# Linear-attention denominators: one per chunk on the whole array, or four at once in column quarters with the reciprocals spread through DRAM

## The chip, the cores and the metric

The kernel runs on one core of a Trainium2 chip. The metric is the device time of one execution in microseconds. The kernel before took 1658.59 us (median of three runs, 1658.3 to 1659.22).

## The reference

Four layers run on x of 2048 rows by 1024: attention, gated block, attention, gated block. Each layer normalizes x without weights and adds its result to x. An attention layer computes, for 32 heads of 32 columns:

```
phi = lambda t: jnp.where(t > 0, t + 1, jnp.exp(t)) + 1e-6
pq, pk = phi(q), phi(k)
kv = jnp.einsum("bhsd,bhse->bhde", pk, v)
z = jnp.einsum("bhsd->bhd", pk)
num = jnp.einsum("bhqd,bhde->bhqe", pq, kv)
den = jnp.einsum("bhqd,bhd->bhq", pq, z)[..., None] + 1e-6
o = num / den          # then o @ wo
```

So each row and head has one denominator, the dot product of its 32 values of phi(q) with the 32 sums z of its head. A gated block computes (x @ w_gate) * (x @ w_up) @ w_down with an inner width of 3584. Weights and activations are bf16.

## The kernel before

X stays on the chip as 16 tiles of 128 rows. An attention layer has two stages. The k/v stage computes phi(k) and v for all rows and sums k-transposed times v in PSUM, with a column of ones that gives z. Behind it `finish_kv` cuts out the four 32 by 32 head blocks of each 128-column chunk with `mask`, writes z into the same block pattern as `zb` (128 x 128 per chunk), and `fold` multiplies the blocks with wo, so that the output projection and the numerator become one product with M.

The q stage is a written-out order of steps i, and it is the part that changes. A q chunk is 128 columns of q (four heads) for a group of 512 rows; there are four groups of eight chunks, 32 in all. Per step the code issues, in this order:

- `den_step` (L283) for chunk i - 4: one matmul of the chunk's `zb` with its phi(q), whose 128 output rows are each head's denominator 32 times over (`dps`); logarithm and exponential with scale -1 on ScalarE give the reciprocal `r` (L288, L289); a multiplication on VectorE gives the scaled chunk `pqs` (L292);
- `q_step` (L272) for chunk i: eight matmuls, then `phi` (L171): an exponential on ScalarE, two steps on VectorE;
- in the steps 4 to 11 one `fold` (two matmuls, one copy of M on ScalarE, one on VectorE);
- from step 12 on an `out_step` (L294): eight matmuls of the scaled chunks of a group with M, and an addition to X on VectorE.

Every engine takes its instructions in the order of the code. Products of q and output steps share four PSUM tiles (`mm`), folds and denominators three (`kv`). SyncE's queue issues the loads of the gated block's weights where `preload_B` is called (steps 0, 14, 17, 25, 33), as slots come free, and the transposes of the next layer's first rows. The gated block (L356) follows at once.

Of the kernel before, what the change touches and what calls it, by code (L numbers as in the profile page):

```python
# [9 lines left out]
ALU = mybir.AluOpType  # L10
BF16 = mybir.dt.bfloat16
F32 = mybir.dt.float32
# [3 lines left out]
def kernel(  # L16
# [11 lines left out]
    nc = tc.nc  # L28
    P = 128
# [3 lines left out]
    KD = D // P  # L33
    KF = F // P
    G = 512
    NG = S // G
    TPG = G // P
    NB = 512
    FB = F // NB
    FPB = NB // P  # L40
    DC = D // NB
    HC = 7

    ctx.enter_context(tc.manual_schedule())

# [3 lines left out]
    wp = ctx.enter_context(tc.tile_pool(name="wp", bufs=13))  # L49
    hp = ctx.enter_context(tc.tile_pool(name="hp", bufs=4))  # L50
    work = ctx.enter_context(tc.tile_pool(name="work", bufs=2))
    psum = ctx.enter_context(tc.tile_pool(name="psum", bufs=4, space=bass.MemoryType.PSUM))

    x_view = A_x[0].rearrange("(t p) d -> p t d", p=P)
# [51 lines left out]
    nc.gpsimd.memset(mask[:], 0.0)  # L106
    for b in range(4):
        nc.gpsimd.memset(mask[32 * b:32 * b + 32, 32 * b:32 * b + 32], 1.0)
    eps5 = const.tile([P, 1], F32, tag="eps5", name="eps5")
    nc.gpsimd.memset(eps5[:], 1e-5)  # L110
    eps6 = const.tile([P, 1], F32, tag="eps6", name="eps6")
# [59 lines left out]
    def phi(ps, dst):  # L171
        m = work.tile([P, NB], F32, tag="m", name="m", bufs=3)
        nc.scalar.activation(out=m[:], in_=ps[:], func=ACT.Exp)  # L173
        nc.vector.tensor_scalar(out=m[:], in0=m[:], scalar1=1.0, scalar2=1e-6, op0=ALU.min, op1=ALU.add)  # L174
        nc.vector.scalar_tensor_tensor(out=dst, in0=ps[:], scalar=0.0, in1=m[:], op0=ALU.max, op1=ALU.add)

    def layer_A(li, preload_B):
# [55 lines left out]

        kvm = work.tile([P, KD, P], BF16, tag="kvm", name="kvm", bufs=1)
        kvT = work.tile([P, KD, P], BF16, tag="kvT", name="kvT", bufs=1)
        zb = work.tile([P, KD, P], BF16, tag="zb", name="zb", bufs=1)
        z = work.tile([P, KD], F32, tag="z", name="z", bufs=1)

        def finish_kv():
            for b in range(3):  # L240
                nb = min(3, KD - 3 * b)
                src = kvp[b][:, 0:nb * VW].rearrange("p (c f) -> p c f", f=VW)
                nc.vector.tensor_copy(out=z[:, 3 * b:3 * b + nb], in_=src[:, :, P])
                for j in range(nb):
                    nc.vector.tensor_tensor(out=kvm[:, 3 * b + j, :], in0=src[:, j, 0:P], in1=mask[:], op=ALU.mult)
            for c in range(KD):
                nc.vector.tensor_scalar(out=zb[:, c, :], in0=mask[:], scalar1=z[:, c:c + 1], scalar2=None,
                                        op0=ALU.mult)

        def tr_kv():  # L250
# [15 lines left out]
                else:  # L266
                    nc.vector.tensor_copy(out=M[n][:, c, :], in_=ps[:])

        pq = {}
        pqs = {}  # L270

        def q_step(g, c):  # L272
            xnT = xnTs[(li, g)]
            w = wA["q"][c // (NB // P)]
            j = c % (NB // P)
            ps = mm_tile()
            for k in range(KD):
                nc.tensor.matmul(out=ps[:], lhsT=w[:, k, j * P:(j + 1) * P], rhs=xnT[:, k, :],  # L278
                                 start=(k == 0), stop=(k == KD - 1))
            pq[(g, c)] = work.tile([P, G], BF16, tag="pq", name="pq", bufs=6)  # L280
            phi(ps, pq[(g, c)][:])

        def den_step(g, c):  # L283
            p = pq.pop((g, c))
            dps = kv_tile("dps")
            nc.tensor.matmul(out=dps[:], lhsT=zb[:, c, :], rhs=p[:], start=True, stop=True)  # L286
            r = work.tile([P, G], F32, tag="r", name="r", bufs=2)
            nc.scalar.activation(out=r[:], in_=dps[:], func=ACT.Ln, bias=eps6[:], scale=1.0)  # L288
            nc.scalar.activation(out=r[:], in_=r[:], func=ACT.Exp, scale=-1.0)  # L289
            if c % 4 == 0:  # L290
                pqs[(g, c // 4)] = hp.tile([P, HC, G], BF16, tag="h", name="pqs")
            nc.vector.tensor_tensor(out=pqs[(g, c // 4)][:, c % 4, :], in0=p[:], in1=r[:], op=ALU.mult)  # L292

        def out_step(g, j):  # L294
            tl, n = divmod(j, DC)
            t = g * TPG + tl
            ps = mm_tile("ops")
            for c in range(KD):
                nc.tensor.matmul(out=ps[:], lhsT=pqs[(g, c // 4)][:, c % 4, tl * P:(tl + 1) * P],  # L299
                                 rhs=M[n][:, c, :], start=(c == 0), stop=(c == KD - 1))  # L300
            nc.vector.tensor_tensor(out=X[:, t, n * NB:(n + 1) * NB], in0=X[:, t, n * NB:(n + 1) * NB],
                                    in1=ps[:], op=ALU.add)

        LAG, OLAG = 4, 12
        NQ = NG * KD
        for i in range(NQ + OLAG):
            if i >= LAG and i - LAG < NQ:
                den_step(*divmod(i - LAG, KD))
            if i < NQ:
                q_step(*divmod(i, KD))  # L310
            if i == 0:
                for t in range(NT - TPG, NT):
                    kp(t)
                finish_kv()
                preload_B("p")
            if i == 3:
                tr_kv()
            if 4 <= i < 4 + KD:
                fold(i - 4)
            if i >= OLAG:  # L320
                out_step(*divmod(i - OLAG, KD))
            if i in (14, 17, 25, 33):
                preload_B({14: "pr", 17: "r", 25: "r", 33: "rrr"}[i])
            for u in range(TPG):
                if i == 20 + 2 * u:
                    ln_stats(li + 1, (u,))
                if i == 21 + 2 * u:
                    ln_norm(li + 1, u)
                if i == 22 + 2 * u:
                    tr_tile(li + 1, u)  # L330
# [25 lines left out]
    def layer_B(li, stream):  # L356
        last = li == 3
        for g in range(NG):
            xnT = xnTs[(li, g)]
            hT = []  # L360
            nl, ng = (li, g + 1) if g + 1 < NG else (li + 1, 0)
            for f in range(KF):
                fb, j = divmod(f, FPB)
                if j == 0:
                    wg, wu = stream.have.pop((g, fb))
                gp = mm_tile("gp")
                for k in range(KD):
                    nc.tensor.matmul(out=gp[:], lhsT=wg[:, k, j * P:(j + 1) * P], rhs=xnT[:, k, :],  # L368
                                     start=(k == 0), stop=(k == KD - 1))
                up = mm_tile("up")  # L370
                for k in range(KD):
                    nc.tensor.matmul(out=up[:], lhsT=wu[:, k, j * P:(j + 1) * P], rhs=xnT[:, k, :],  # L372
                                     start=(k == 0), stop=(k == KD - 1))
                gs = work.tile([P, NB], F32, tag="gs", name="gs", bufs=2)
                nc.scalar.copy(out=gs[:], in_=gp[:])  # L375
                if f % HC == 0:
                    hT.append(hp.tile([P, HC, G], BF16, tag="h", name="hT"))
                nc.vector.tensor_tensor(out=hT[f // HC][:, f % HC, :], in0=gs[:], in1=up[:], op=ALU.mult)  # L378
                if j == FPB - 1:
                    stream.pair()  # L380
                    stream.rows()
                for u in range(TPG if nl < 4 else 0):
                    t = ng * TPG + u
                    if f == 6 + 4 * u:
                        ln_stats(nl, (t,))
                    if f == 7 + 4 * u:
                        ln_norm(nl, t)
                    if f == 8 + 4 * u:
                        tr_tile(nl, t)
            xnTs.pop((li, g))  # L390
            if g == NG - 1 and not last:
                wA["k"] = load_A(1)
                wA["v"] = load_A(2)
                wA["q"] = load_A(0)
                wA["o"] = load_wo()
            for tl in range(TPG):
                t = g * TPG + tl
                for n in range(DC):
                    ps = kv_tile("dn")
                    for f in range(KF):  # L400
                        nc.tensor.matmul(out=ps[:], lhsT=hT[f // HC][:, f % HC, tl * P:(tl + 1) * P],  # L401
                                         rhs=stream.wd[f // 4][:, f % 4, n * NB:(n + 1) * NB],
                                         start=(f == 0), stop=(f == KF - 1))
                    nc.vector.tensor_tensor(out=X[:, t, n * NB:(n + 1) * NB], in0=X[:, t, n * NB:(n + 1) * NB],  # L404
                                            in1=ps[:], op=ALU.add)
                    if last:
                        nc.sync.dma_start(out=o_view[:, t, n * NB:(n + 1) * NB], in_=X[:, t, n * NB:(n + 1) * NB])
# [40 lines left out]
```

## Time and profile before

| what | value |
|---|---|
| median of three runs | 1658.59 us (1658.3 to 1659.22) |
| profiled execution, its own time | 1658.14 us |
| its span, first to last instruction | 1656.3 us |
| TensorE busy | 1644.8 us, 99% |
| VectorE busy | 558.8 us, 34% |
| ScalarE busy | 367.8 us, 22% |
| DMA packets, share of 16 engines | 35.9% |
| granted TensorE clock | 1.000 |

A group row of the profile names the line, the engine, the operation, output and inputs with their sizes, and the count; behind the first bar stand the busy time in us and the mean ns of one; behind the second the idle time of that engine just before these instructions, and what ended it. A matmul's own duration overlaps the next one's, so the pitch from start to start is shorter than the mean of one. In a row of the chain of waits stand the start in us, the length, and the work. In a row of windows stand, per engine, busy time and instructions, then the granted clock, the busy share of the DMA engines and GB/s. SPq is SyncE's queue.

### The profile page before, as it was taken

The numbers are of one execution on the slowest core, as the hardware profiler recorded it, in microseconds if no ns is written. First come the engines' busy times: TensorE is split into PE (matmuls) and PEld (weight loads), VectorE is DVE, ScalarE is ACT, GpSimd is POOL, SyncE is SP. The second block draws the span as 40 slices with busy tenths as digits, with TensorE's granted clock in tenths as the row PEclk, the third lists the DMA queues.
The fourth block names the chain that finished last, engine by engine and source line by source line (L and its number), as shares of the span: only waits on it lengthen the run. The fifth ranks groups of instructions, "written<-read, shape, count | busy, mean of one in ns | idle before, by whom it ended". The sixth has DMA issues, their size and how long they took to land.

```text
span 1656.3 us, 18423 instructions
## 1 busy us (share of the span) xinstructions
PE 1644.8 (99%) x7824; PEld 754.9 (46%) x7824; DVE 558.8 (34%) x982; ACT 367.8 (22%) x695; POOL 1.6 (0%) x17
## 2 busy tenths in 40 slices
PE   8999999999999999999999999999999999999999
PEld 3544444444444444444444444444444444444444
DVE  5547762311321231132156288522113212211111
ACT  4336541100110110011033375311001101100110
POOL 0000000000000000000000000000000000000000
PEclk9999999999999999999999999999999999999999
DMA  6432034630461264056141221346225504622400
GB/s 222 134 77 101 17 112 134 171 128 21 140 165 56 83 172 127 20 139 166 57 102 35 81 89 45 118 134 171 80 89 147 162 30 134 172 81 89 153 29 23
DMA packets 210866, 174.21 MB, mean 105 GB/s; under 512 B 66400, under 2 KB 201568, under 8 KB 210784
## 3 DMA queue, kind: packets, MB, share of 16 engines
q1 hardware_dynamic: 210784, 173.03, 35.9%
q8 instruction: 61, 1.00, 0.2%
q14 instruction: 21, 0.17, 0.0%
HBM read 153.09 MB, written 4.19 MB: 95 GB/s over the span
## 4 chain that ended last, share of the span: by engine, by line
PE 99%; DMA 0%; SPq 0%; DVE 0%; issue 0%
PE dn L401 23%; PE up L372 23%; PE gp L368 23%; PE ps L187 14%; PE ps L278 7%; PE ops L299 7%; PE kvp L203 1%; PE dps L286 1%; DMA wk<-in_A_wqkv_dram 0%; PE mps L263 0%; PE pt L162 0%; PE pt L253 0%; SPq L65 0%; DVE X L404 0%
## 5 line engine op out<-in xcount | busy, mean ns | idle before, releaser
L368 PE MATMUL gp<-xnT,wg 128*128 128x512 bf16 x1792 | 423.3, 379 | 0.0
L372 PE MATMUL up<-xnT,wu 128*128 128x512 bf16 x1792 | 423.3, 379 | 0.0
L401 PE MATMUL dn<-wd,hT 128*128 128x512 bf16 x1792 | 388.1, 379 | 0.0
L378 DVE TENSOR_TENSOR hT<-gs,up 128x512 bf16<-128x512 f32 x224 | 154.0, 688 | 567.0 <-PE up L372 567.0
L375 ACT COPY gs<-gp 128x512 f32<-128x512 f32 x224 | 131.3, 586 | 945.9 <-PE gp L368 945.9
L368 PEld LDWEIGHTS <-wg 128*128 128x128 bf16 x1792 | 175.4, 98 | 211.4
L401 PEld LDWEIGHTS <-hT 128*128 128x128 bf16 x1792 | 175.4, 98 | 211.4
L372 PEld LDWEIGHTS <-wu 128*128 128x128 bf16 x1792 | 175.3, 98 | 211.5
L404 DVE TENSOR_TENSOR X<-X,dn 128x512 bf16<-128x512 bf16 x64 | 44.0, 687 | 342.2 <-PE dn L401 342.2
L187 PEld LDWEIGHTS <-xnT 128*128 128x128 bf16 x1024 | 100.4, 98 | 121.8 <-issue 2.9
L278 PE MATMUL ps<-xnT,wq 128*128 128x512 bf16 x512 | 120.3, 379 | 0.0
L299 PE MATMUL ops<-M,pqs 128*128 128x512 bf16 x512 | 118.3, 379 | 0.0
L187 PE MATMUL ps<-wk,xnT 128*128 128x512 bf16 x512 | 115.6, 384 | 1.6 <-DMA wk<-in_A_wqkv_dram 1.6
L187 PE MATMUL ps<-wv,xnT 128*128 128x512 bf16 x512 | 111.8, 379 | 0.0
L173 ACT ACTIVATE m<-ps 128x512 f32<-128x512 f32 x128 | 76.3, 596 | 156.3 <-PE ps L187 128.3
L135 DVE BATCH_NORM_STATS2 st<-X 128x6 f32<-128x512 bf16 x128 | 81.8, 681 | 3.8 <-DMA X<-in_A_x_dram 3.8
L174 DVE TENSOR_SCALAR m<-m 128x512 f32<-128x512 f32 x128 | 54.1, 422 | 84.1 <-ACT m L173 83.5
L299 PEld LDWEIGHTS <-pqs 128*128 128x128 bf16 x512 | 50.1, 98 | 60.4
L278 PEld LDWEIGHTS <-wq 128*128 128x128 bf16 x512 | 50.0, 98 | 60.1 <-issue 0.6
L288 ACT ACTIVATE r<-dps,eps 128x512 f32<-128x512 f32 x64 | 44.3, 692 | 54.1 <-PE dps L286 54.1
L292 DVE TENSOR_TENSOR pqs<-pq,r 128x512 bf16<-128x512 bf16 x64 | 43.8, 685 | 31.4 <-ACT r L289 31.4
L196 ACT CAST vb<-ps 128x512 bf16<-128x512 f32 x64 | 37.7, 588 | 65.2 <-PE ps L187 65.2
(37 smaller groups left out, 373.5 us busy)
## 6 DMA issues: line engine op xcount, KB each, us to landing
wg<-in_B_w_gate_dram SPq DMA_DIRECT2D x56, 1024.0 KB, 5.2
wu<-in_B_w_up_dram SPq DMA_DIRECT2D x56, 1024.0 KB, 6.7
wd<-in_B_w_down_dram SPq DMA_DIRECT2D x14, 1024.0 KB, 5.5
X<-in_A_x_dram SPq DMA_DIRECT2D x16, 256.0 KB, 7.7
wk<-in_A_wqkv_dram SPq DMA_DIRECT2D x4, 1024.0 KB, 7.0
wv<-in_A_wqkv_dram SPq DMA_DIRECT2D x4, 1024.0 KB, 8.9
wq<-in_A_wqkv_dram SPq DMA_DIRECT2D x4, 1024.0 KB, 7.2
wo<-in_A_wo_dram SPq DMA_DIRECT2D x4, 1024.0 KB, 8.6
```

Of the source, the lines that this page charges most:

```text
L135: nc.vector.bn_stats(out=st[:, c, :], in_=X[:, t, c * FMAX:(c + 1) * FMAX])
L173: nc.scalar.activation(out=m[:], in_=ps[:], func=ACT.Exp)
L174: nc.vector.tensor_scalar(out=m[:], in0=m[:], scalar1=1.0, scalar2=1e-6, op0=ALU.min, op1=ALU.add)
L187: nc.tensor.matmul(out=ps[:], lhsT=xnT[:, k, tl * P:(tl + 1) * P], rhs=w[:, k, :], start=(k == 0), stop=(k == KD - 1))
L278: nc.tensor.matmul(out=ps[:], lhsT=w[:, k, j * P:(j + 1) * P], rhs=xnT[:, k, :], start=(k == 0), stop=(k == KD - 1))
L288: nc.scalar.activation(out=r[:], in_=dps[:], func=ACT.Ln, bias=eps6[:], scale=1.0)
L299: nc.tensor.matmul(out=ps[:], lhsT=pqs[(g, c // 4)][:, c % 4, tl * P:(tl + 1) * P], rhs=M[n][:, c, :], start=(c == 0), stop=(c == KD - 1))
L368: nc.tensor.matmul(out=gp[:], lhsT=wg[:, k, j * P:(j + 1) * P], rhs=xnT[:, k, :], start=(k == 0), stop=(k == KD - 1))
L372: nc.tensor.matmul(out=up[:], lhsT=wu[:, k, j * P:(j + 1) * P], rhs=xnT[:, k, :], start=(k == 0), stop=(k == KD - 1))
L375: nc.scalar.copy(out=gs[:], in_=gp[:])
L378: nc.vector.tensor_tensor(out=hT[f // HC][:, f % HC, :], in0=gs[:], in1=up[:], op=ALU.mult)
L401: nc.tensor.matmul(out=ps[:], lhsT=hT[f // HC][:, f % HC, tl * P:(tl + 1) * P], rhs=stream.wd[f // 4][:, f % 4, n * NB:(n + 1) * NB], star ...
```

## The change

Four chunks make a quad. `zb` shrinks to 32 columns per chunk, eight for each of its four heads (`hmask`). `den_quad` issues four matmuls with 32 output rows each, one to each column quarter of the array, into one PSUM tile; one logarithm and one exponential then give the reciprocals of four chunks. Every eighth row of `r` (16 rows: four chunks j by four heads h) is written to a DRAM tile `rd` ordered by head, then chunk. `spread` reads it back: each head's four rows of 512 numbers go to the 32 partitions of that head, for all four chunks, 128 partitions by 8 KB. Both transfers are issued on ScalarE's queue. `scale` multiplies a chunk of phi(q) in place with its part of `rb`.

In the order of steps, quad u is computed at the start of step 4u+5 (before, chunk i at step i+4), spread behind the q chunk of step 4u+6, and its chunks scaled behind the q chunk of step 4u+8 (two) and at the start of step 4u+9 (two). Output steps begin at step 14 instead of 12. phi(q) is kept seven chunks to a tile. `r` and `rb` have one buffer. The gated block's `gs` shares the buffers of `m`.

```
-        zb = work.tile([P, KD, P], BF16, tag="zb", name="zb", bufs=1)
+        zb = work.tile([P, KD, HW], BF16, tag="zb", name="zb", bufs=1)
...
-        def den_step(g, c):
-            p = pq.pop((g, c))
+        def den_quad(u):
             dps = kv_tile("dps")
-            nc.tensor.matmul(out=dps[:], lhsT=zb[:, c, :], rhs=p[:], start=True, stop=True)
-            r = work.tile([P, G], F32, tag="r", name="r", bufs=2)
+            for j in range(4):
+                i = 4 * u + j
+                nc.tensor.matmul(out=dps[HW * j:HW * j + HW, :], lhsT=zb[:, i % KD, :], rhs=pq_at(i),
+                                 start=True, stop=True, tile_position=(0, HW * j))
+            r = work.tile([P, G], F32, tag="r", name="r", bufs=1)
             nc.scalar.activation(out=r[:], in_=dps[:], func=ACT.Ln, bias=eps6[:], scale=1.0)
             nc.scalar.activation(out=r[:], in_=r[:], func=ACT.Exp, scale=-1.0)
-            if c % 4 == 0:
-                pqs[(g, c // 4)] = hp.tile([P, HC, G], BF16, tag="h", name="pqs")
-            nc.vector.tensor_tensor(out=pqs[(g, c // 4)][:, c % 4, :], in0=p[:], in1=r[:], op=ALU.mult)
+            rd = dramp.tile([4, 4, G], F32, tag="rd", name="rd")
+            nc.scalar.dma_start(out=rd[:].rearrange("h j n -> j h n"), in_=r[0:P:8, :])
+            rbs[u] = rd
+
+        def spread(u):
+            rd = rbs[u]
+            rb = work.tile([P, 4, G], F32, tag="rb", name="rb", bufs=1)
+            nc.scalar.dma_start(out=rb[:].rearrange("p j n -> p (j n)"),
+                                in_=rd[:].rearrange("h j n -> h (j n)").unsqueeze(1).to_broadcast([4, HW, 4 * G]))
+            rbs[u] = rb
+
+        def scale(i):
+            nc.vector.tensor_tensor(out=pq_at(i), in0=pq_at(i), in1=rbs[i // 4][:, i % 4, :], op=ALU.mult)
...
-        LAG, OLAG = 4, 12
+        OLAG = 14
         NQ = NG * KD
         for i in range(NQ + OLAG):
-            if i >= LAG and i - LAG < NQ:
-                den_step(*divmod(i - LAG, KD))
+            if i % 4 == 1 and 8 <= i < NQ + 8:
+                for j in (2, 3):
+                    scale(i - 9 + j)
+            if i % 4 == 1 and 5 <= i < NQ + 5:
+                den_quad(i // 4 - 1)
             if i < NQ:
-                q_step(*divmod(i, KD))
+                q_step(i)
+            if i % 4 == 2 and 6 <= i < NQ + 6:
+                spread(i // 4 - 1)
+            if i % 4 == 0 and 8 <= i < NQ + 8:
+                for j in (0, 1):
+                    scale(i - 8 + j)
...
-                gs = work.tile([P, NB], F32, tag="gs", name="gs", bufs=2)
+                gs = work.tile([P, NB], F32, tag="m", name="gs", bufs=3)
```

What stands where now. ScalarE, in the middle of the q stage before (line numbers of the kernel before): exponential of a q chunk (L173), then logarithm and exponential of a denominator (L288, L289), step after step.

```order
L173 ACTIVATE m<-ps 128x512
L288 ACTIVATE r<-dps,eps_117 128x512
L289 ACTIVATE r<-r 128x512
L173 ACTIVATE m<-ps 128x512
L288 ACTIVATE r<-dps,eps_117 128x512
L289 ACTIVATE r<-r 128x512
```

ScalarE at the same place of the changed kernel (its own line numbers: L179 is the exponential of a q chunk, L301 and L302 those of a quad, L304 the write to DRAM, L310 the spread):

```order
L304 DMA rd<-r 4x4x512
L179 ACTIVATE m<-ps 128x512 x2
L310 DMA rb<-rd 128x1x2048
L179 ACTIVATE m<-ps 128x512 x2
L301 ACTIVATE r<-dps,eps_125 128x512
L302 ACTIVATE r<-r 128x512
L304 DMA rd<-r 4x4x512
```

Two exponentials of q chunks stand between a write and its spread, and two between the spread and the next quad. VectorE in the changed kernel, around the scaling of the fifth quad (L180 and L181 are the two steps of phi, L325 the addition to X, L316 the scaling, L141 and L142 the statistics of the next layer):

```order
L180 TENSOR_SCALAR m<-m 128x512
L181 SCALAR_TENSOR_TENSOR pq<-ps,m 128x512
L316 TENSOR_TENSOR pq<-pq,rb 128x512 x2
L325 TENSOR_TENSOR X<-X,ops 128x512
L141 BN_STATS st<-X 128x6 x2
L142 BN_AGGR mv<-st 128x2
L316 TENSOR_TENSOR pq<-pq,rb 128x512 x2
L180 TENSOR_SCALAR m<-m 128x512
L181 SCALAR_TENSOR_TENSOR pq<-ps,m 128x512
L325 TENSOR_TENSOR X<-X,ops 128x512
```

An addition to X, and here the statistics, stand between the two pairs of scalings, and phi and the additions of the following steps stand behind them. Before, each step had one scaling (L292) between an addition to X and the phi of the next chunk.

More of the change, by code (lines that the diff above doesn't have):

```diff
@@ L42 @@
     HC = 7
+    HW = 32
     ctx.enter_context(tc.manual_schedule())
@@ L51 @@
     work = ctx.enter_context(tc.tile_pool(name="work", bufs=2))
+    dramp = ctx.enter_context(tc.tile_pool(name="dramp", bufs=4, space=bass.MemoryType.DRAM))
     psum = ctx.enter_context(tc.tile_pool(name="psum", bufs=4, space=bass.MemoryType.PSUM))
@@ L108 @@
         nc.gpsimd.memset(mask[32 * b:32 * b + 32, 32 * b:32 * b + 32], 1.0)
+    hmask = const.tile([P, HW], F32, tag="hmask", name="hmask")
+    nc.gpsimd.memset(hmask[:], 0.0)
+    for b in range(4):
+        nc.gpsimd.memset(hmask[32 * b:32 * b + 32, 8 * b:8 * b + 8], 1.0)
     eps5 = const.tile([P, 1], F32, tag="eps5", name="eps5")
@@ L246, in finish_kv @@
             for c in range(KD):
-                nc.vector.tensor_scalar(out=zb[:, c, :], in0=mask[:], scalar1=z[:, c:c + 1], scalar2=None,
+                nc.vector.tensor_scalar(out=zb[:, c, :], in0=hmask[:], scalar1=z[:, c:c + 1], scalar2=None,
                                         op0=ALU.mult)
@@ L267, in fold, with pq_at, q_step @@
                     nc.vector.tensor_copy(out=M[n][:, c, :], in_=ps[:])
-        pq = {}
         pqs = {}
-        def q_step(g, c):
+        rbs = {}
+        def pq_at(i):
+            if i // HC not in pqs:
+                pqs[i // HC] = hp.tile([P, HC, G], BF16, tag="h", name="pq")
+            return pqs[i // HC][:, i % HC, :]
+        def q_step(i):
+            g, c = divmod(i, KD)
             xnT = xnTs[(li, g)]
@@ L279, in q_step @@
                                  start=(k == 0), stop=(k == KD - 1))
-            pq[(g, c)] = work.tile([P, G], BF16, tag="pq", name="pq", bufs=6)
-            phi(ps, pq[(g, c)][:])
-        def den_step(g, c):
-            p = pq.pop((g, c))
+            phi(ps, pq_at(i))
+        def den_quad(u):
             dps = kv_tile("dps")
-            nc.tensor.matmul(out=dps[:], lhsT=zb[:, c, :], rhs=p[:], start=True, stop=True)
-            r = work.tile([P, G], F32, tag="r", name="r", bufs=2)
+            for j in range(4):
[3 more added lines that the diff above has]
+            r = work.tile([P, G], F32, tag="r", name="r", bufs=1)
             nc.scalar.activation(out=r[:], in_=dps[:], func=ACT.Ln, bias=eps6[:], scale=1.0)
             nc.scalar.activation(out=r[:], in_=r[:], func=ACT.Exp, scale=-1.0)
-            if c % 4 == 0:
-                pqs[(g, c // 4)] = hp.tile([P, HC, G], BF16, tag="h", name="pqs")
-            nc.vector.tensor_tensor(out=pqs[(g, c // 4)][:, c % 4, :], in0=p[:], in1=r[:], op=ALU.mult)
+            rd = dramp.tile([4, 4, G], F32, tag="rd", name="rd")
[7 more added lines that the diff above has]
+            rbs[u] = rb
+            rbs[u] = rb
+        def scale(i):
+            nc.vector.tensor_tensor(out=pq_at(i), in0=pq_at(i), in1=rbs[i // 4][:, i % 4, :], op=ALU.mult)
         def out_step(g, j):
@@ L298, in out_step @@
             for c in range(KD):
-                nc.tensor.matmul(out=ps[:], lhsT=pqs[(g, c // 4)][:, c % 4, tl * P:(tl + 1) * P],
+                nc.tensor.matmul(out=ps[:], lhsT=pq_at(g * KD + c)[:, tl * P:(tl + 1) * P],
                                  rhs=M[n][:, c, :], start=(c == 0), stop=(c == KD - 1))
```

## The prediction

> **What bounds the kernel now.** I read the page's first two parts, then the chain of work that ended last, then the table of windows and the list of DMA issues.
>
> ```profile
> span 1656.3 us, 18423 instructions
> PE 1644.8 (99%) x7824; PEld 754.9 (46%) x7824; DVE 558.8 (34%) x982; ACT 367.8 (22%) x695; POOL 1.6 (0%) x17
> PE 99%; DMA 0%; SPq 0%; DVE 0%; issue 0%
> ```
>
> TensorE sets the time from end to end, so a TensorE slot that goes away shortens the run, provided no wait takes its place. The stage that changes is the q stage, once per attention layer. Its chain in the first layer:
>
> ```profile
> 144.01 1.73 PE ps L278 x8
> 145.74 0.43 PE mps L263 x2
> 146.17 0.22 PE dps L286
> 146.38 1.73 PE ps L278 x8
> ...
> 161.71 0.22 PE dps L286
> 161.92 1.73 PE ps L278 x8
> 163.65 1.73 PE ops L299 x8
> ...
> 237.47 15.54 PE ops L299 x72
> ```
>
> A q chunk and an output step take 1.73 us each, eight matmuls at 0.216 us; a fold of two takes 0.43, a denominator 0.22. The row at 144.01 is q chunk 6; it ends at 145.74, and the last output step of the layer at 237.47 + 15.54 = 253.01. So 107.3 us lie between, without a gap on TensorE. The other engines' pieces there:
>
> ```profile
> L286 PE MATMUL dps<-pq,zb 128*128 128x512 bf16 x64 | 24.2, 379 | 0.1
> L286 PEld LDWEIGHTS <-zb 128*128 128x128 bf16 x64 | 6.3, 98 | 7.3
> L173 ACT ACTIVATE m<-ps 128x512 f32<-128x512 f32 x128 | 76.3, 596 | 156.3 <-PE ps L187 128.3 <-PE ps L278 27.2
> L174 DVE TENSOR_SCALAR m<-m 128x512 f32<-128x512 f32 x128 | 54.1, 422 | 84.1 <-ACT m L173 83.5
> L175 DVE SCALAR_TENSOR_TENSOR pq<-ps,m 128x512 bf16<-128x512 f32 x64 | 44.3, 692 | 2.2
> L288 ACT ACTIVATE r<-dps,eps 128x512 f32<-128x512 f32 x64 | 44.3, 692 | 54.1 <-PE dps L286 54.1
> L289 ACT ACTIVATE r<-r 128x512 f32<-128x512 f32 x64 | 40.3, 629 | 2.0
> L292 DVE TENSOR_TENSOR pqs<-pq,r 128x512 bf16<-128x512 bf16 x64 | 43.8, 685 | 31.4 <-ACT r L289 31.4
> L301 DVE TENSOR_TENSOR X<-X,ops 128x512 bf16<-128x512 bf16 x64 | 43.9, 686 | 16.1 <-PE ops L299 16.1
> L267 DVE CAST M<-mps 128x512 bf16<-128x512 f32 x16 | 10.9, 680 | 0.0
> L135 DVE BATCH_NORM_STATS2 st<-X 128x6 f32<-128x512 bf16 x128 | 81.8, 681 | 3.8 <-DMA X<-in_A_x_dram 3.8
> L136 DVE BATCH_NORM_AGGREGATE mv<-st 128x2 f32<-128x12 f32 x64 | 13.4, 209 | 2.2
> ```
>
> **The change part by part.** *TensorE.* 64 denominator slots of 0.216 us (0.865 us per four chunks) become 16 quads. A matmul of a column quarter stands nowhere in this trace. From below, all four stream together: 0.22 us per quad. From above, one after another (0.865) with the array emptied before and after: 379 ns of one less the 216 ns pitch is 163 ns, plus an uncovered load of 98 ns, twice: 1.39 us. I take 0.5: together, and one such gap of 0.26. That would be 16 x 0.365 = 5.8 us less, at most 10.3, or 8.4 more. The Trainium skill, "TensorEngine Tiling (Array Packing)", Key Properties, says that changing the tiling mode drains TensorE, which speaks against the 0.22; no run here shows it yet.
>
> *ScalarE and VectorE.* Logarithm and exponential run 16 times, not 64 (ScalarE is 22% busy: nothing on the path). The 64 scalings stay at 685 ns, since their types stay; they now wait for the spread transfer, and behind them on VectorE stand the additions to X and the phi steps that free TensorE's four product tiles. Behind a spread that waits on ScalarE stand the exponentials of the next chunks. The single buffer of r costs nothing (the write that reads it is over four steps before the next quad), nor do the seven chunks to a tile and gs in the buffers of m, which gets three where it had two. The output lag of 14 only changes the order of the same output steps.
>
> *The transfers*, two per quad. The write of 32 KB is bounded by the store row below, 1.7 us. It is covered: two q chunks lie between it and the spread. The spread reads 32 KB and writes 1 MB:
>
> ```profile
> wg<-in_B_w_gate_dram SPq DMA_DIRECT2D x56, 1024.0 KB, 5.2
> wd<-in_B_w_down_dram SPq DMA_DIRECT2D x14, 1024.0 KB, 5.5
> out_dram<-X SPq DMA_DIRECT2D x32, 128.0 KB, 1.7
> ...
> 158.00:162.00 4.00, 4.00 (x21) 1.78 (x19) 3.93 (x8) 2.57 (x6) 0.00 (x0) 1.00 0.68 239
> 162.00:166.00 4.00, 4.00 (x20) 1.84 (x19) 2.77 (x5) 2.24 (x4) 0.00 (x0) 1.00 0.81 286
> ```
>
> The last two numbers of a window are DMA share and GB/s: 286 / 0.81 and 239 / 0.68 are both about 352 GB/s at full share, 22 per engine. A megabyte on 16 engines is thus 3.0 us of data in 5.2, and 2.2 us are fixed. Every transfer of the kernel before has 128 partitions as its outermost extent. The spread's source has four rows outermost, each repeated 32 times, and I expect it to be divided by those four: four engines, 256 KB each, 12.0 us of data, **14.2 us** to land. From below the landing time is 5.2 us (16 engines); No row has a source like it; I take the upper end, since four is what the source offers to be divided. The Trainium skill, "DMA: Bandwidth & Descriptors", section on why a DMA increments its semaphore by 16, states such a rule: the engine count is the largest number up to 16 that divides the slowest extents of both sides, here 4 of (4, 128). No run here shows it. By that page's 27 GiB/s per engine the data would take an estimated 9.0 us, the landing 11.2 and the run 1722.
>
> *What is late next.* There is one buffer rb, so ScalarE issues spread u+1 only once VectorE has done all four scalings of quad u. With a landing time L the quads form a chain of their own, and I add it from the end of q chunk 6:
> - to the first spread: the exponential 0.6 and 0.2 between engines, 0.8 us;
> - eight landings, 8 L;
> - between two landings four scalings of 0.685 and 0.1: 2.84. Behind quad 0 a copy of M (0.68) stands between the pairs, from quad 2 on an addition to X (0.69), at quads 3 and 4 statistics as well (2 x 0.68 + 0.21 = 1.57). The seven sum to 19.88 + 0.68 + 5 x 0.69 + 2 x 1.57 = 27.15;
> - after the last landing four scalings and an addition, 3.43, a last matmul 0.3 with its wait, and seven output steps, 12.1.
>
> Sum 43.8 + 8 L. Before it was 107.3, and by then TensorE has lost three denominators for one quad, 0.15 early. Each layer grows by 8 L - 63.6. At 14.2 that is 50 us. The chain decides as long as its cycle, L + 3.5, exceeds TensorE's own four steps, 4 x 3.46 + 0.5 = 14.3, that is, for L over 10.8. In this regime the quad's price is hidden: TensorE waits at the output steps, either for the scaled chunk or for its product tile, and the saving of 5.8 is gone.
>
> On top come SP's weight loads, on the same engines:
>
> ```profile
> 148.18 0.37 SPq L72 DMA_DIRECT2D wu<-in_B_w_up_dram  x1
> 157.85 0.92 SPq L78 DMA_DIRECT2D wd<-in_B_w_down_dram  x2
> 204.61 0.53 SPq L78 DMA_DIRECT2D wd<-in_B_w_down_dram  x1
> 219.28 11.37 SPq L78 DMA_DIRECT2D wd<-in_B_w_down_dram  x3
> ```
>
> Seven megabytes per layer lie in the stage. Each is 3.0 us on the four engines if it falls into a spread: between 0 and 21 us per layer. I take 6, three megabytes at two thirds, for the load behind q chunk 7 and the last two fall surely into a flight, and two queues may fill one engine better than one.
>
> Sum: 2 x (50 + 6) = 112 on the span of 1656.3, 1768. The profiled execution took 1658.14, 1.8 beside its span: **1770 us**. (The median of the runs shown is 1658.59, 0.45 above the profiled one.)
>
> **The rivals.**
> *A: sixteen engines, faster.* If the spread is divided by its 128 destination rows it lands in 5.2 to 5.9 us. In the body it is then hidden: a spread is issued 0.8 us after q chunk 4u+6, and VectorE comes to the scaling 2.0 us after chunk 4u+8 (exponential 0.60, the two steps of phi 0.42 and 0.69, and 0.3 between engines), which is 5.5 us later in the fold steps of 2.16 us and 8.1 later where a step is 3.46. At the end it isn't: from the start of the last quad to its dps 0.66, logarithm and exponential 1.4, write 1.7, spread 5.5, scalings and addition 3.43, together 12.7; TensorE has the quad, five output steps and seven matmuls, 10.7. So 2.1 us of waiting per layer, about 4.4 in both. The run is faster if 16 x (0.865 - quad) passes 4.4 + 3.3 (0.2% of the run, about what a measurement here can tell from no change): a quad below 0.38 us. At 0.3: 9.0 - 4.4, a time of 1654. For it: the destination has 128 rows. Against: four source rows. Chance 0.10.
> *B: sixteen engines, no change.* The same with a quad of about 0.5: 5.8 - 4.4, a time of 1657. Chance 0.09.
> *C: sixteen engines, and the quarters don't run together*, so that the change doesn't do what it says: a quad of 1.39 costs 8.4, with 4.4 at the end 1671. Chance 0.05.
>
> **How the numbers follow.** The forecast, four engines and a chain of spreads, has 0.76. Its own range: with L = 11, 8 L - 63.6 = 24 per layer and 3 of contention, 1712; with 14.2 and all 21, 1800; slower descriptors would add 16 per microsecond of L. So 1710 to 1810. The rivals lie between 1652 and 1671 and hold 0.24; the range over all starts at 1656, which takes in B and C and leaves A and the far end out: 1656 to 1810. Faster by over 0.2%: 0.10 (A). Within 0.2%: 0.09 (B). Slower: 0.81 (forecast and C).
>
> **What would show it.** The issue list: rb<-rd lands in 11 us or more (forecast) or 5 to 6 (rivals). The scalings on VectorE show idle time before them whose releaser is the DMA into rb, some 100 us in sum with 16 spreads; TensorE's idle time stands before the output steps and, in the fold steps, before the folds, whose product tiles VectorE frees. ScalarE waits at the spread for VectorE. The DMA line's bytes grow by 16 MB, its share little. The group of dps shows the quad: four rows starting within 0.1 us of each other, or 0.216 apart. The prediction is wrong if rb lands in under 8 us, and its chain is wrong if landings are long and TensorE doesn't wait at the output steps.

## The result: 1851 us, 11.6% slower, and the profile after

The changed kernel took 1850.98 us (median of four runs, 1849.81 to 1854.95) against 1658.76 before: 1.116 times the time, 95% interval 1.1146 to 1.1177. The forecast was 1770, with 1810 as its upper end. The direction and the place were as forecast; the amount was not.

The page of the changed kernel: the span, the engines, the DMA queues (q1 is SyncE's, q10 ScalarE's; the last number is the share of 16 engines' span that the packets took), the chain of waits, and three groups.

```profile
span 1848.4 us, 18358 instructions
PE 1682.3 (91%) x7824; PEld 757.1 (41%) x7824; DVE 553.1 (30%) x982; ACT 307.3 (17%) x599; POOL 2.1 (0%) x22
q1 hardware_dynamic: 210784, 173.03, 36.7%
q10 hardware_dynamic: 2432, 17.30, 3.8%
PE 79%; DMA 18%; DVE 3%; issue 0%; SPq 0%; ACT 0%
L323 PE MATMUL ops<-M,pq 128*128 128x512 bf16 x512 | 144.0, 434 | 127.3 <-DVE X L325 69.3 <-DVE pq L316 58.0
L316 DVE TENSOR_TENSOR pq<-pq,rb 128x512 bf16<-128x512 bf16 x64 | 40.9, 683 | 201.6 <-DMA rb<-rd 201.6
L298 PE MATMUL dps<-pq,zb 128*32 128x512 bf16 x64 | 6.4, 389 | 1.5 <-ACT M L271 1.5
```

TensorE was 99% of the chain; now 18% of it is DMA, nearly all of that one transfer, rb<-rd. VectorE sat 201.6 us before the scalings waiting for rb, and TensorE 127.3 us before the output steps, waiting for the additions to X (which free its product tiles) and for scaled chunks. The chain of waits of the first layer, start and length in us:

```profile
141.12 0.33 PE dps L298 x4
141.45 1.83 PE ps L290 x8
...
145.54 20.10 DMA rb<-rd
...
168.80 23.38 DMA rb<-rd
...
192.20 2.50 DVE pq L316 x4
...
194.74 18.32 DMA rb<-rd
...
216.21 20.26 DMA rb<-rd
...
241.01 18.84 DMA rb<-rd
...
264.40 19.18 DMA rb<-rd
...
286.72 23.00 DMA rb<-rd
...
312.87 18.17 DMA rb<-rd
```

Eight transfers in a row, each issued when VectorE has scaled the quad before, TensorE nowhere between them. Their sum is 161.25 us here, 161.98 in the other attention layer. The third and the last, with no other load beside them, land in 18.2 us; the first, second and seventh, with one or two weight loads beside them, in 20 to 23. A single landing scatters: the fourth took 20.3 with nothing beside it.

### The profile page after: what moved, and what is told of

Its sections match the earlier page's. It is cut to its first block, busy times and chain, and to the rows that moved or that the text cites. A ratio compares the mean times of both kernels' runs of the same rounds, so it can differ in the third digit from the quotient of the medians.

```text
span 1848.4 us, 18358 instructions
## 1 busy us (share of the span) xinstructions
PE 1682.3 (91%) x7824; PEld 757.1 (41%) x7824; DVE 553.1 (30%) x982; ACT 307.3 (17%) x599; POOL 2.1 (0%) x22
## 3 DMA queue, kind: packets, MB, share of 16 engines
q10 hardware_dynamic: 2432, 17.30, 3.8%
## 4 chain that ended last, share of the span: by engine, by line
PE 79%; DMA 18%; DVE 3%; issue 0%; SPq 0%; ACT 0%
PE dn L433 21%; PE up L404 21%; PE gp L400 21%; DMA rb<-rd 17%; PE ps L193 12%; DVE pq L316 2%; PE ops L323 2%; PE ps L290 1%; PE kvp L209 1%; DMA wk<-in_A_wqkv_dram 0%; DVE X L325 0%; DVE st L141 0%; PE pt L168 0%; PE mps L269 0%; DVE M L273 0%
## 5 line engine op out<-in xcount | busy, mean ns | idle before, releaser
L323 PE MATMUL ops<-M,pq 128*128 128x512 bf16 x512 | 144.0, 434 | 127.3 <-DVE X L325 69.3
L323 PEld LDWEIGHTS <-pq 128*128 128x128 bf16 x512 | 54.2, 106 | 209.1 <-issue 95.1
L290 PE MATMUL ps<-xnT,wq 128*128 128x512 bf16 x512 | 133.9, 411 | 0.3
L179 ACT ACTIVATE m<-ps 128x512 f32<-128x512 f32 x128 | 76.3, 596 | 299.0 <-PE ps L290 163.5
L316 DVE TENSOR_TENSOR pq<-pq,rb 128x512 bf16<-128x512 bf16 x64 | 40.9, 683 | 201.6 <-DMA rb<-rd 201.6
L180 DVE TENSOR_SCALAR m<-m 128x512 f32<-128x512 f32 x128 | 53.8, 420 | 108.8 <-ACT m L179 107.9
L141 DVE BATCH_NORM_STATS2 st<-X 128x6 f32<-128x512 bf16 x128 | 81.8, 680 | 3.9 <-DMA X<-in_A_x_dram 3.9
L325 DVE TENSOR_TENSOR X<-X,ops 128x512 bf16<-128x512 bf16 x64 | 43.3, 681 | 18.6 <-PE ops L323 18.4
```

The source lines that it names most:

```text
L141: nc.vector.bn_stats(out=st[:, c, :], in_=X[:, t, c * FMAX:(c + 1) * FMAX])
L316: nc.vector.tensor_tensor(out=pq_at(i), in0=pq_at(i), in1=rbs[i // 4][:, i % 4, :], op=ALU.mult)
L323: nc.tensor.matmul(out=ps[:], lhsT=pq_at(g * KD + c)[:, tl * P:(tl + 1) * P], rhs=M[n][:, c, :], start=(c == 0), stop=(c == KD - 1))
```

## The experiments

Labels e and f are two sets; each kernel is the changed one with the edit shown, and is compared with the kernel before at 1658 to 1659 us. For a landing I give the third and the last of the first layer, where no weight load runs beside it, unless it says otherwise.

**How many engines work: 16 source rows.**

```
-            rd = dramp.tile([4, 4, G], F32, tag="rd", name="rd")
-            nc.scalar.dma_start(out=rd[:].rearrange("h j n -> j h n"), in_=r[0:P:8, :])
+            rd = dramp.tile([16, 4, G], F32, tag="rd", name="rd")
+            nc.scalar.dma_start(out=rd[:].rearrange("h j n -> j h n"), in_=r[0:P:2, :])
...
-   .unsqueeze(1).to_broadcast([4, HW, 4 * G])
+   .unsqueeze(1).to_broadcast([16, 8, 4 * G])
```

> Edit: four copies of each head's reciprocals are written to DRAM (64 rows for 16), and the one 1 MB spread reads them as 16 rows, each repeated 8 times, in place of 4 rows repeated 32 times. Same bytes, same 8 KB pieces, same queue, same order. Theory T (the source's outermost extent sets how many of the 16 DMA engines work; four of them gave 16.5 GB/s each in the changed kernel): 16 engines, 64 KB each, lands in 5 to 7 us, the waits for rb at the scalings in the middle of the stage vanish, 2 to 3 us per layer stay at the end, time 1652 to 1662 us. Rival R1 (the engines are all at work, and the 8 KB pieces, the DRAM round trip or ScalarE's queue are slow): landing stays near 20 us, time near 1850 us.

1679.54 us, ratio 1.0122 (1.0105 to 1.0139). The landing fell from 18.2 to 7.4 us, which refutes R1; the time is 17 us above the most that theory T gave. Parts of the chain, first layer:

```profile
144.01 3.33 DMA rd<-r
...
147.41 7.43 DMA rb<-rd
...
234.71 5.81 DMA rd<-r
...
240.59 7.31 DMA rb<-rd
```

In the middle of the stage no transfer is left in the chain. Two spreads remain in this layer: the first, among the folds, and the last, behind which TensorE has only output steps that need it. In the second layer the second quad's spread remains as well (7.16 us at 1002.25). The write had not been expected: 128 KB instead of 32, and 5.8 us at the end, where weight loads ran beside it (261 GB/s in the window from 234 to 240 us).

**Eight source rows**, the same edit with 8 for 16 and 16 repeats (every fourth row of r is written).

> The same with 8 source rows, each repeated 16 times (two copies of each head written). Theory T: 8 engines, 128 KB each at 16.5 GB/s, 7.9 us and 2.2 fixed: lands in 9.5 to 11 us; the chain 8 L - 63.6 is then just at TensorE's own pace: time 1670 to 1710 us. R1: 20 us, 1850 us.

1726.06 us (one run, as all that follow without an interval). The landing of the first layer's last spread:

```profile
259.96 10.72 DMA rb<-rd
```

4, 8 and 16 rows: 18.2, 10.7 and 7.3 us in the last flight of the layer, for the same megabyte in the same 8 KB pieces. The traces show it without the times too: where the spread is alone, the DMA share is 0.25 with 4 rows (317 to 321 us), 0.52 with 8 (262 to 269) and 0.95 with 16 (242 to 246), that is, 4, 8 and 15 to 16 of the 16 engines. So the number of source rows sets how many engines work. The time is 16 us above the expected span, as loaded landings took up to 15.1 us.

**Two buffers for rb.**

```
-            rb = work.tile([P, 4, G], F32, tag="rb", name="rb", bufs=1)
+            rb = work.tile([P, 4, G], F32, tag="rb", name="rb", bufs=2)
-    mask = const.tile([P, P], F32, tag="mask", name="mask")
+    mask = const.tile([P, P], BF16, tag="mask", name="mask")     # hmask likewise
```

> Edit: rb gets two buffers (mask and hmask become bf16 to make room); the transfer with 4 source rows stays. Theory T with its chain (a spread is issued only once the quad before it is scaled): the next transfer is issued while the last one is still waited for, so landings follow each other by the transfer's data time or TensorE's progress, about 17.5 us in place of 21.6; 15 to 30 us less per layer, time 1790 to 1825 us, each transfer not faster from its start on the engines. Rival R2 (the single buffer is no part of the cycle; only the transfer's own time counts against each quad's slack): 1845 to 1855 us.

1823.78 us: 27 us of the 192 come back, at the small end of what was expected. The single buffer was part of the cycle, and the transfer's own time the larger part: VectorE still waited 175.6 us for rb. The chain of this run also has writes rd<-r of 12.5 and 13.4 us (at 154.10 and 288.56), issued while a spread was in flight; the next spread waits for its write, so the transfers still follow one another.

**Pieces of 2 KB.**

```
-            nc.scalar.dma_start(out=rb[:].rearrange("p j n -> p (j n)"), in_=...)
+            for j in range(4):
+                nc.scalar.dma_start(out=rb[:, j, :], in_=rd[:, j, :].unsqueeze(1).to_broadcast([4, HW, G]))
```

> Edit: the spread as four transfers of 256 KB, one per chunk, each from 4 rows of 2 KB repeated 32 times. Still 4 source rows, but pieces of 2 KB as in the weight loads. Theory P (four engines, and 16.5 GB/s for 22 because a piece is 8 KB into one partition): the four together land in about 15 us, time near 1775 us. Theory Q (four engines give 16.5 GB/s whatever the piece): 18 to 20 us for the last, time 1840 to 1865 us.

1763.32 us. The queue row, and the issue of the first of the four pieces and the landing of the fourth, last quad of the first layer:

```profile
q10 hardware_dynamic: 8768, 17.30, 3.1%
```
```profile
276.99 0.53 ACTq L311
...
278.65 12.63 DMA rb<-rd
```

The 12.63 us count from the fourth issue. From the first, at 276.99, the megabyte landed in 14.3 us (14.6 in the third flight), where one piece took 18.2. Four engines again (DMA share 0.26), the same bytes, a fifth less time. The queue rows point the same way without the chain, loaded landings included: 17.30 MB over 3.8% of 16 engines' 1848.4 us are 15.4 GB/s per working engine in the changed kernel, over 3.1% of 1761.5 us 19.8 GB/s here. Theory P stands for these rows.

**Does repetition, a fresh write or the rows' distance matter?** Four kernels. In three of them the reciprocals are left out: the spread fetches rows of w_gate into a bf16 rb, so that only the times are of use (their scalings take 0.42 us, not 0.69, so their totals don't compare with the changed kernel's, the landings do). First, 128 different rows of 7 KB:

```
+   in_=B_w_gate[0:132].rearrange("(a b) n -> a b n", b=33)[:, 0:HW, :]
```

> Edit: the spread of the changed kernel reads 4 blocks of 32 different rows of w_gate (7 KB each, 896 KB in all) in place of 4 rows 32 times; 4 is still the outermost extent. This leaves the reciprocals out (weights stand in their place, in bf16) and the spread no longer reads what was just written. Theory P (a long piece into one partition is what slows an engine to 15 or 16 GB/s): 229 KB per engine at 15.4 GB/s and 2.2 fixed, lands in 16.5 to 18 us, time 1805 to 1845 us. Rival R3 (reading the same rows again and again, or right after they were written, slows it): about 22 GB/s, lands near 12.7 us, time 1740 to 1775 us.

```profile
186.87 13.72 DMA rb<-in_B_w_gate_dram
...
280.78 13.59 DMA rb<-in_B_w_gate_dram
```

1778.70 us, below what P gave and nearer to R3 (at the same two places of the second layer the landings were 15.5 and 16.3). But this run changed three things: the size, the repetition and the origin of the rows. So the next two took 8 KB rows of w_gate, once 128 different ones, once 4 repeated 32 times.

> Edit: the spread of the changed kernel reads 128 different rows of 8 KB (4 blocks of 32, from w_gate taken flat) in place of 4 rows 32 times; the reciprocals are left out, as in the run with the 7 KB rows, which landed in 13.7 us where no other load was under way (18.2 in the changed kernel). Theory P2 (a piece of 8 KB is the cost, whichever rows it comes from): 17.5 to 18.5 us in the undisturbed landings. Theory R3 (the repeated rows are the cost): 15 to 16 us (13.7 less 2.2, times 8/7, and 2.2 again).

> Edit: as the one before, but 4 rows of w_gate, 264 KB apart, each repeated 32 times; nothing in the transfer was written before. Reciprocals left out. P2: 17.5 to 18.5 us. R3 by repetition: 17.5 to 18.5 us. R3 by the fresh write (rows that were just written to DRAM are slow to read) or by the 8 KB between the four rows: 15 to 16 us.

Different rows, then repeated ones (third and last landing):

```profile
191.50 15.54 DMA rb<-in_B_w_gate_dram
...
296.99 16.62 DMA rb<-in_B_w_gate_dram
```
```profile
188.62 16.78 DMA rb<-in_B_w_gate_dram
...
288.54 15.76 DMA rb<-in_B_w_gate_dram
```

1805.35 and 1802.76 us, landings of 16.1 and 16.3 on average. Reading the same rows again and again costs nothing that these runs show. Neither theory had its value in the first of them: 16.1 lies above R3's end and below P2's. The 2 us that remain to 18.2 go with the origin of the rows: w_gate against the tile rd that was just written. Four rows 8.75 KB apart instead of 8:

> Edit: the changed kernel with the four DRAM rows 8.75 KB apart in place of 8 KB, all else the same. If the four engines get in each other's way because their rows lie a power of two apart: 13.5 to 16 us. If not: 18 to 18.5 us undisturbed, time 1845 to 1855 us.

1844.09 us, landings of 18.14 and 17.95: the distance of 8 KB isn't it. Whether the fresh write or the place of rd in DRAM (four rows close together) costs those 2 us stays open. Neither does it alone: 2 KB pieces came from the same fresh rd and landed in 14.3 to 14.6.

**Half the bytes.** Reciprocals in bf16, four rows of 4 KB:

> Edit: the changed kernel with the reciprocals in bf16: 4 rows of 4 KB repeated 32 times, 512 KB. If a piece of 4 KB goes at the rate of the 2 KB pieces (1 MB in 12.5 us undisturbed): 7 to 8 us for the half, time 1675 to 1700 us. If at that of the 8 KB pieces: 10 to 10.5 us, time 1690 to 1715 us.

1682.42 us; the shortest landing in the chain was 7.67 us, most with a load beside them 10.5 to 10.9. The queue's 8.65 MB over 1.6% of 1680.6 us are 20.1 GB/s per engine: 4 KB pieces go at the rate of 2 KB ones.

**Toward a version that beats both.** With 16 rows, and the last quad of each layer done chunk by chunk on the whole array as before (`ALONE` is (7,) here; `den_one` is the old den_step with a wide zb for those chunks):

```
+            if 4 <= i < NQ + 4 and (i - 4) // 4 in ALONE:
+                den_one(i - 4)
-            if i % 4 == 1 and 5 <= i < NQ + 5:
+            if i % 4 == 1 and 5 <= i < NQ + 5 and i // 4 - 1 not in ALONE:
```

> Edit: 16 source rows as in the run with 16 rows, and the last quad of each layer is computed chunk by chunk on the whole array as before (lag 4), so that no spread stands at the end of the stage. Theory T (in the run with 16 rows two spreads per layer are left uncovered, the first one among the folds and the last one, where write, landing and scalings cost 8 to 9 us): 16 to 19 us less than 1679.5, that is, 1660 to 1665 us. Rival R4 (what is left is spread over the middle of the stage, by contention with the weight loads): 1672 to 1680 us.

1659.97 us: 19.6 less than with all eight spreads. Most of what the 16 rows left was at the end of the layer, none of it in the middle; R4 falls. Two spreads per layer stay in the chain, early in the stage (at 146.23 and 171.59 in the first). Then the reciprocals in bf16 as well:

```
-            nc.scalar.activation(out=r[:], in_=r[:], func=ACT.Exp, scale=-1.0)
+            rh = work.tile([P, G], BF16, tag="rh", name="rh", bufs=1)
+            nc.scalar.activation(out=rh[:], in_=r[:], func=ACT.Exp, scale=-1.0)
```

> Edit: as the run without the last spread, and the reciprocals go to DRAM and back in bf16: half the bytes, pieces of 4 KB. Theory T: landing 4.5 to 5.5 us, so that the first spread is covered too; what stays is the quads' gain on TensorE, 7 quads in 2 layers at 0.865 less 0.43 (0.33 for the four, 0.10 lost by the next matmul) = 6.1 us: 1650 to 1656 us. R4: above 1665 us.

1654.07 us (1652.86 to 1654.33), ratio 0.997 (0.9959 to 0.9982) to the kernel before. A group and the chain around a quad and at the end of the first layer:

```profile
L330 DVE TENSOR_TENSOR pq<-pq,rb 128x512 bf16<-128x512 bf16 x56 | 20.7, 415 | 0.0
```
```profile
171.87 0.33 PE dps L303 x4
172.20 1.83 PE ps L295 x8
...
231.46 18.99 PE ops L337 x88
250.45 1.73 PE gp L416 x8
```

VectorE waits for rb no more, the scaling takes 415 ns instead of 685 now that both inputs are bf16, and the gated block starts at 250.45 where it started at 253.01. That is 2.56 us per layer; 7 quads at 0.865 less 0.43 would be 3.0, and the rest is lost among the folds. This version differs from the run before it in bytes, piece size and scaling at once, so the share of each isn't told apart. With the first quad of each layer chunk by chunk too:

> Edit: as the one before, with the first quad of each layer also chunk by chunk. Theory T: if the first spread still cost something there, that goes, against 0.43 us of TensorE per layer: 1650 to 1655 us. If it was covered, about 1 us slower than the one before.

1654.56 us, ratio 0.9975 (0.9965 to 0.9984): the same within the intervals.

## Why the prediction was right in its chain and wrong in its size

**The engines: right.** Four source rows, four engines; 4, 8 and 16 rows show it, with DMA shares of 0.25, 0.52 and 0.95. The rule cited from the Trainium skill, "DMA: Bandwidth & Descriptors", in the section on why a DMA increments its semaphore by 16, agrees with these runs. All three rivals needed 16 engines and fell with that.

**The chain: right.** Its working gave a growth of 8 L - 63.6 per layer. With the measured landings in place of 8 L, that is 161.25 - 63.6 and 161.98 - 63.6, together 196.0 us; the span grew by 192.1. With the landings of the run with 8 rows (99.6 and 98.8 us in sum) the same formula gives 71 us for a growth of 68. Part of this closeness is luck, since its other terms err in both directions. Too much: between the landings of a layer VectorE took 24.3 us for 27.15 (four scalings in a row 2.50, the row at 192.20, for 2.74), and the first spread was issued 0.1 us behind q chunk 6 and not 0.8, beside the exponential and not after it. Too little: from the last landing to the end of the layer it was 18.1 and 17.3 us for 15.8, because the output steps began at a lower clock (last section). TensorE waits where it was said to, at the output steps, and the quad's price is hidden.

**The landing time: the step that failed.** The prediction took 14.2 us, from 22 GB/s per engine, and its range left only 0.6 us above it (1810 less 1800, at 16 us per microsecond of L). That rate came from windows in which weights move in pieces of 1 and 2 KB; the spread writes 8 KB in one piece to each partition. 4 x 3.0 us of data were really 16.0 (18.2 less the 2.2 fixed), 16.4 GB/s per engine; the queue row, with the loaded landings in it, gives 15.4. With 2 KB pieces the same four engines landed the megabyte from the same rows in 14.3 to 14.6 us, so the term was right for the piece that it was taken from, and that run, at 1763 us, came near the forecast of 1770. With 8 KB pieces of weight rows it was 16.1 to 16.3. So the whole 4 us appear only where both come together, the long piece and the rows of rd. The size of the piece could be read from the change, and the prediction touched it only as "slower descriptors". 4.0 us too little per landing, sixteen landings: 64 us.

**The weight loads: undersized.** Landings beyond 18.2 sum to 161.25 - 8 x 18.2 = 15.7 us in the first layer and 16.4 in the second. The prediction took 6 of its bounds 0 and 21: 20 us too little. Not all of it is weights. Of the 32.0 us of both layers, 25.4 lie in the three landings of each layer with weight loads beside them, 3.2 in the four beside the transposes of the next layer's rows, and 3.5 in the other six, for which the traces show no cause. Both terms together, 84, on the forecast span of 1768 make 1852; it was 1848.4.

**The quad: the middle of the range.** 0.5 us was taken of 0.22 to 1.39. The rows at 141.12 and 141.45 show 0.33 for the four and 0.10 more in the next chunk: 0.43. The quarters do stream together. The array doesn't stand empty for 0.26 us on either side, but 0.21 of the 0.43 is more than one stream; the rule of the Trainium skill, "TensorEngine Tiling (Array Packing)", Key Properties, that a change of mode drains the array, fits that, and these rows don't prove it.

**Rival A** had the end of the layer at 2.1 us of waiting with 16 engines. With 16 rows it was more: landing 7.3 and write 5.8, where 5.5 and 1.7 had been put in (the write carried four times the bytes of A's). In the version where the last spread is gone and the bytes are halved, the small gain that A described appears, 4.8 us of time.

## What to carry to other kernels

For a transfer that repeats a few rows over many partitions, look at the outermost extent of both sides first: with 4 rows there, a megabyte took 18 us, with 16 rows 7 us. Take a rate from rows whose pieces are as long as yours and whose source is like yours, and let the upper bound of an unknown include a worse rate than any row shows. A prefetch with one buffer, issued in the order of an engine that also waits for its consumer, turns its latency into a cycle: eight times the latency, and the saving on the busiest engine (here 7 us of slots) disappears behind it; at the end of a stage, where nothing is left to hide it, do without.

## What the runs showed that was not expected

*Long pieces from rd are slow.* By the queue rows, 8 KB pieces went at 15.4 GB/s per engine from rd and at 17.6 from w_gate, 2 and 4 KB pieces from rd at 19.8 and 20.1. These rows take in loaded flights. In windows of 9 to 14 us in the middle of the first layer's third, fourth and last flight, where almost nothing else moves and the DMA share is 0.24 to 0.26, the four engines together moved:

| source and piece | GB/s |
|---|---|
| rd, 8 KB (the changed kernel) | 64 to 69 |
| w_gate, 8 KB (different and repeated rows) | 76 to 85 |
| w_gate, 7 KB | 83 to 87 |
| rd, 4 KB (bf16; a window of 5 us in the last flight) | 90 |
| rd, 2 KB | 88 to 91 |

So the length of a piece alone doesn't make it slow: from w_gate, 8 KB pieces are little slower than 7 KB ones. What it is about long pieces from rd isn't shown.

*The clock falls while TensorE waits.* Windows around the last spread of the first layer in the changed kernel; the third number from the end is the granted clock:

```profile
317.00:321.00 4.00, 0.92 (x5) 0.20 (x2) 0.00 (x0) 0.00 (x0) 0.00 (x0) 1.00 0.25 63
325.00:329.00 4.00, 0.00 (x0) 0.00 (x0) 0.00 (x0) 0.00 (x0) 0.00 (x0) 0.50 0.19 63
336.00:339.00 3.00, 3.00 (x9) 1.07 (x8) 0.69 (x1) 0.00 (x0) 0.00 (x0) 0.50 0.00 0
339.00:342.00 3.00, 3.00 (x15) 1.31 (x14) 0.69 (x1) 0.00 (x0) 0.00 (x0) 0.97 0.00 0
```

And the chain behind it:

```profile
333.61 15.51 PE ops L323 x58
```

After some us of waiting the clock is at half, and it stays there until about 339, five us after the output steps have begun again. The 58 matmuls from 333.61 on take 15.51 us where 58 x 0.216 would be 12.5: the long wait at the end costs 3 us more than its own length (2 in the second layer, where they take 14.69). Elsewhere in the stage the slow matmuls lie beside a transfer that takes longer anyway.
